# Similarity products of clustered attention: 32 instead of 128 columns of the centroids' tile

## The chip, the cores and the metric

One core of one Trainium2 chip. The metric is the device time in microseconds (us) of one execution; the median of three runs of the kernel before is 679.25 us (678.80 to 679.58).

## The reference

The model is clustered attention followed by two feed-forward blocks, all in float32. Batch 2, 8 heads, 768 tokens, head size 64, 16 centroids for each head.

```python
c_n = centroids / (norm(centroids) + 1e-06)
q_assign = argmax(einsum('bhsd,hcd->bhsc', q_n, c_n), axis=-1)
k_assign = argmax(einsum('bhsd,hcd->bhsc', k_n, c_n), axis=-1)
mask = q_assign[:, :, :, None] == k_assign[:, :, None, :]
scores = where(mask, scale * q @ k.T, -1e9)
attn = softmax(scores); attn_out = attn @ v
```

A token thus takes part only in the attention of its own cluster. The change touches only the products `q @ c_n` and `k @ c_n`, from which the largest of 16 similarities is picked. After the attention come a Fourier mixing over tokens and channels, a normalization, an MLP of width 2048, and a gated MLP of width 1024 with a convolution of three taps.

## The kernel before, in words

**Stages.** Attention fills the first 250 us or so of the span. The mixing of batch 0 and the first weights are woven into it; the MLPs follow, with the mixing of batch 1 beside them. The 16 head-batch pairs are taken two at a time: `m` (0 to 7) numbers the pairs, and one `raw` tile holds q and k of two heads, 64 partitions each.

**Order of the work.** The attention runs in an order written out by hand. A loop over steps `n` (L856) issues a score step for the maximum (`score_max`, L587 and L589: four matmuls of 384 columns), a second computation of the same scores for the exponential (`score_exp`, L624 and L626, four more), the product with V (`attn_v`, L664, 18 short matmuls), and whatever the dictionaries `pre`, `mid`, `late`, `aft`, `post` and `fill` list for that step. TensorE takes its matmuls in that order. Three PSUM slots (`slot`, L363) go round between score steps and everything else.

**The similarity products.** The tile `W` (L400) has 128 partitions, four pairs of heads and 128 columns. It is set to zero, and L424 and L425 copy the normalized centroids of one head into columns 0 to 15 (partitions 0 to 63) and those of the other head into columns 16 to 31 (partitions 64 to 127). Columns 32 to 127 stay zero. `prep_sims` (L442) makes twelve float32 matmuls for a pair: the stationary operand is a block of 128 tokens of q or k, the moving operand is `W[:, m % 4, :]`, and product `t` writes 128 columns of PSUM from column `32 * t`. The next product overwrites all but the first 32 of them, so that columns 0 to 383 end up with the similarities of the twelve blocks. `prep_equal` (L451) reads just those. In the trace a float32 matmul stands as two weight loads and two matmuls, 24 of each for one call.

**When.** Pairs 0 and 1 are done back to back before the loop (L836, L845). The transposes of the first head's mask follow (`first_mask`, L490, matmuls at L495), then the first score steps. `prep_sims` of pairs 2 to 7 is listed in `post` (L690), one call in every twelve steps. Its result goes through VectorE (L455, L457), GpSimd (L461) and VectorE again (L465, L471), back to TensorE to be turned (L483), and by DMA into the stacked operands of a later head. No DMA is issued by `prep_sims`.

**Other lines that the steps below touch.** `keep_warm` (L406) multiplies zeros and nothing reads its result: eight such matmuls of 512 columns stand ahead of the centroids' work (L410), two behind the transpose of the centroids (L422), and four at step -2 (L716). `scales` (L334) has the only other float32 matmuls with 32 moving columns or fewer; `first_max` (L612) turns the maxima of the first head.

Of the kernel before, what the change touches and what calls it, by code (L numbers as in the profile page):

```python
# [49 lines left out]
def tile_net(ctx, tc, qk, v, cen, w12, w34, conv, dft, odd, out):  # L50
    nc = tc.nc
    V, A, G, T = nc.vector, nc.scalar, nc.gpsimd, nc.tensor
# [302 lines left out]
    with ExitStack() as actx:  # L355
# [7 lines left out]
        def slot(name):  # L363
            turn[0] = (turn[0] + 1) % 3
            return ps.tile([128, 2, 512], F32, tag=f"s{turn[0]}", bufs=1, name=name)
# [34 lines left out]
        W = ep.tile([128, 4, 128], F32, name="W")  # L400
        V.memset(W, 0.0)
        t = slot("warm_up")
# [27 lines left out]
        for i in range(2):  # L430
            t = ap.tile([128, NT, 2, 130], F16, name=f"V16_{i}")
# [6 lines left out]
        def first_bank(name):  # L438

            return ps.tile([128, 512], F32, tag="av", bufs=2, name=name)  # L440

        def prep_sims(m):  # L442
            raw = raws[m]
            sm = sims[m] = first_bank("sim1") if m == 1 else slot(f"sim{m}")[:, 0]
            for t in range(12):
                T.matmul(sm[:, 32 * t:32 * t + 128], raw[:, t // 6, (t % 6) * 128:(t % 6) * 128 + 128],
                         W[:, m % 4, :], start=True, stop=True)
            if m != 1:
                prep_equal(m)

        def prep_equal(m):  # L451
            sm = sims[m]
            sv = sm[:, 0:384].rearrange("p (g h c) -> p h g c", g=12, h=2)
            mx = ep.tile([128, 2, 12], F32, tag="mx", bufs=1, name=f"mx{m}")
            V.tensor_reduce(mx, sv, AX.X, ALU.max)  # L455
            eq = eqs[m] = ep.tile([128, 24, C], F16, tag="eq", bufs=1, name=f"eq{m}")
            V.tensor_tensor(eq.rearrange("p (h g) c -> p h g c", h=2), sv,  # L457
                            mx.unsqueeze(3).to_broadcast([128, 2, 12, C]), ALU.is_equal)
# [227 lines left out]
        for m in range(1, NH // 2):  # L686
            k = 12 * m - 24
            if m > 1:
                at(pre, k, load_raw, m)
                at(post, k + 5, prep_sims, m)  # L690
                at(fill, k + 6, prep_first, m, V if m == 6 else G)
                at(fill, k + 7, prep_pick, m)
                at(fill if m == 7 else late, k + (7 if m == 7 else 8), prep_mark, m)
                at(fill, k + 8, prep_hi, m, (0,))
                at(fill, k + (9 if m < 7 else 8), prep_lo, m, 0, G if m < 7 else V)
                at(fill, k + (9 if m < 7 else 8), prep_hi, m, (1,))
                at(mid, k + 11, prep_turn, m)
                at(fill, k + (10 if m < 7 else 9), prep_lo, m, 1, G if m < 7 else V)
            turn_v = {1: 7, 6: 66, 7: 72}.get(m, k + 15)
            load, top, hi, lo = {1: (2, 5, 12, 13), 2: (8, 14, 17, 17), 6: (62, 64, 67, 71), 7: (68, 71, 74, 74)}.get(  # L700
                m, (k + 8, k + 13, k + 17, k + 17))
            at(fill, load, load_v, m)
            at(aft, top, v_max, m)
            at(mid, turn_v, v_turn, m)
            for i in range(4):
                if i:
                    at(aft, turn_v + (1 if 1 < m < 6 else i // 2), v_step, m, i)
                else:
                    at(late, turn_v, v_step, m, i)
            at(fill if m in (1, 6) else aft, hi, v_step, m, 4)  # L710
            at(pre if m == 6 else fill if m == 1 else aft, lo, v_step, m, 5)
# [122 lines left out]
        add_stack(G)  # L834
        first_stack()
        prep_sims(0)  # L836
        for h in range(2):
            parts[h] = stack_parts(h)
# [4 lines left out]
        prep_pick(0)  # L843
        prep_mark(0)
        prep_sims(1)  # L845
        A.copy(Ys[0][0:64, 0], f32(Gs[0][0:64, 0]))
        prep_hi(1)
# [231 lines left out]
    for g in range(B):  # L1079
        for f in range(16):  # L1080
# [7 lines left out]
            if g == 0 and f in (13, 14):  # L1088
                raw = cvs[0].tile([128, 2048], I32, tag="raw64", bufs=2, name=f"junk{f}")
# [102 lines left out]
```

## Time and profile before

| | us |
|---|---|
| Median of 3 runs (lowest, highest) | 679.25 (678.80, 679.58) |
| Profiled execution, device time | 679.98 |
| Span of that execution's profile | 678.2 |
| TensorE matmul (PE) busy | 662.7 (98%) |
| TensorE weight load (PEld) busy | 503.1 (74%) |
| VectorE (DVE) busy | 539.0 (79%) |
| ScalarE (ACT) busy | 417.5 (62%) |
| GpSimd (POOL) busy | 179.1 (26%) |

The device time is 1.78 us more than the span, the part ahead of the first and behind the last instruction. Matmuls are pipelined: the duration of one holds its way through the array as well as the time its columns take, so PE's busy share says little, and the distance between the starts of neighbours says more. PEclk is the granted clock, 1.00 for 2.4 GHz and 0.50 for 1.2 GHz. A bracket behind a row of the timeline gives the idle time of the engine just before it and what ended it.

### The profile page before, as it was taken

How to read it: one execution, taken by the hardware profiler on the slowest of the kernel's cores; microseconds unless marked ns; L12 is line 12 of the kernel's file. 1: busy time of each engine (PE TensorE's matmuls, PEld its weight loads, DVE VectorE, ACT ScalarE, POOL GpSimd, SP SyncE). 2: the span in 40 equal slices, each digit the busy share in tenths (PEclk: the TensorE clock that was granted, in tenths of full speed). 3: DMA queues.
4: the chain of work that ended last, by engine and by line, in shares of the span. 5: the costliest groups of instructions: out<-in, count | busy, mean ns of one | idle time of the engine just before them, and what ended most of it. 6: DMA issues, size and time to landing. Idle time of an engine off the chain costs nothing.

```text
span 678.2 us, 12781 instructions
## 1 busy us (share of the span) xinstructions
PE 662.7 (98%) x5114; PEld 503.1 (74%) x5114; DVE 539.0 (79%) x884; ACT 417.5 (62%) x671; POOL 179.1 (26%) x153
## 2 busy tenths in 40 slices
PE   8999999999999999999999999999999999999997
PEld 6798898988999888999999996555555555555553
DVE  6887889899889999998599848997626399867662
ACT  5577878888667885566246643776436276655442
POOL 8266757678648733000011000000000000000000
PEclk9999999999999999999999999999999999999999
DMA  7657797774643530334113330333000000002002
GB/s 203 166 137 191 187 226 196 199 181 90 170 112 90 140 125 1 126 124 143 45 63 125 125 125 1 124 125 127 1 0 1 1 0 1 1 2 93 1 1 93
DMA packets 21544, 65.42 MB, mean 96 GB/s; under 512 B 4439, under 2 KB 7307, under 8 KB 18669
## 3 DMA queue, kind: packets, MB, share of 16 engines
q1 hardware_dynamic: 20476, 60.86, 31.1%
q0 software_dynamic: 1008, 3.75, 2.0%
q8 instruction: 40, 0.66, 0.4%
q14 instruction: 20, 0.16, 0.1%
HBM read 40.84 MB, written 5.58 MB: 68 GB/s over the span
## 4 chain that ended last, share of the span: by engine, by line
PE 67%; DVE 21%; DMA 4%; ACT 3%; issue 3%; SPq 1%; POOL 1%; DVEq 0%; ACTq 0%
PE acc L87 7%; PE acc L86 7%; PE acc L85 7%; PE up L85 5%; PE up L86 5%; PE up L87 5%; PE av L664 4%; DVE m L592 3%; PE s L587 3%; PE t L624 3%; PE s L589 3%; PE t L626 3%; DVE p L652 3%; PE u L85 2%; PE u L87 2%
## 5 line engine op out<-in xcount | busy, mean ns | idle before, releaser
L652 POOL TENSOR_TENSOR p<-p,p 128x768 f16<-128x768 f32 x61 | 104.6, 1717 | 76.9 <-ACT p L644 35.0
L632 ACT ACTIVATE p<-t,cbias 128x768 f32<-128x768 f32 x93 | 83.6, 900 | 20.1 <-PE t L626 19.5
L592 DVE TENSOR_REDUCE m<-s 128x1 f32<-128x768 f32 x96 | 90.3, 945 | 7.0 <-PE s L589 4.6
L644 ACT CAST p<-p 128x768 f16<-128x768 f32 x90 | 74.7, 830 | 1.4
L664 PE MATMUL av<-V,p 128*128 128x65 f16 x1728 | 70.1, 194 | 1.0 <-POOL p L652 0.9
L664 PEld LDWEIGHTS <-p 128*128 128x128 f16 x1728 | 58.6, 98 | 16.2 <-issue 14.8
L587 PE MATMUL s<-X 128*128 128x384 f32 x192 | 56.1, 373 | 0.5 <-issue 0.4
L624 PE MATMUL t<-X 128*128 128x384 f32 x192 | 53.2, 358 | 0.9 <-DVE m L592 0.6
L589 PE MATMUL s<-Y 96*128 96x384 f32 x192 | 49.7, 340 | 2.1 <-DMA Y<-G 2.1
L626 PE MATMUL t<-Y 98*128 98x384 f32 x192 | 49.4, 338 | 0.0
L85 PE MATMUL u<-x,wb 128*128 128x384 f16 x128 | 41.7, 326 | 1.2 <-DVE h L955 0.8
L85 PE MATMUL up<-un,wa 128*128 128x384 f16 x128 | 41.8, 326 | 0.6 <-DVE x L1034 0.3
L86 PE MATMUL up<-un,wa 128*128 128x384 f16 x128 | 41.7, 326 | 0.0
L87 PE MATMUL u<-x,wb 128*128 128x384 f16 x128 | 41.7, 326 | 0.0
L86 PE MATMUL u<-x,wb 128*128 128x384 f16 x128 | 41.7, 326 | 0.0
L87 PE MATMUL up<-un,wa 128*128 128x384 f16 x128 | 41.6, 326 | 0.0
L652 DVE TENSOR_TENSOR p<-p,p 128x768 f16<-128x768 f32 x32 | 40.2, 1257 | 0.6 <-ACT p L644 0.5
L85 PE MATMUL up<-un,wha 128*128 128x384 f32 x112 | 38.0, 339 | 0.0
L86 PE MATMUL up<-un,wha 128*128 128x384 f32 x112 | 37.8, 338 | 0.0
L87 PE MATMUL up<-un,wla 128*128 128x384 f32 x112 | 37.6, 337 | 0.0
L589 PEld LDWEIGHTS s<-Y 96*128 96x128 f32 x192 | 34.8, 189 | 3.0 <-DMA Y<-G 1.6
L265 POOL TENSOR_TENSOR rs<-rs,half 128x1 f32<-128x1 f32 x12 | 10.5, 900 | 100.6 <-DVE rs L260 92.6
(388 smaller groups left out, 1710.7 us busy)
## 6 DMA issues: line engine op xcount, KB each, us to landing
rawa<-w SPq DMA_DIRECT2D x14, 1024.0 KB, 4.7
rawb<-w SPq DMA_DIRECT2D x8, 1024.0 KB
raw<-qk SPq DMA_DIRECT2D x7, 768.0 KB, 4.2
X<-G SPq DMA_DIRECT2D x13, 384.0 KB, 3.7
Y<-G SPq DMA_DIRECT2D x13, 384.0 KB, 6.8
vraw<-v SPq DMA_DIRECT2D x8, 384.0 KB, 4.9
out<-y SPq DMA_DIRECT2D x12, 256.0 KB, 2.0
X<-G SPq DMA_DIRECT2D x14, 192.0 KB, 4.2
```

The lines of the kernel that those rows point to most:

```text
L85: T.matmul(o, sH, mH, start=start, stop=False)
L86: T.matmul(o, sH, mL, start=False, stop=False)
L87: T.matmul(o, sL, mH, start=False, stop=stop)
L587: T.matmul(t[:, c, 0:384], X[:, 0, sl], X[:, 1, 384 * c:384 * c + 384], start=True, stop=False)
L589: T.matmul(t[:, c, 0:384], Y[0:96, 0, sl], Y[0:96, 1, 384 * c:384 * c + 384], start=False, stop=True)
L592: V.tensor_reduce(m6s[h][:, i:i + 1], t[:, :, 0:384], AX.XY, ALU.max, negate=True)
L624: T.matmul(t[:, c, 0:384], X[:, 1, sl], X[:, 0, 384 * c:384 * c + 384], start=True, stop=False)
L626: T.matmul(t[:, c, 0:384], Y[0:98, 1, sl], Y[0:98, 0, 384 * c:384 * c + 384], start=False, stop=True)
L632: A.activation(p, t[:, :, 0:384], AF.Exp, bias=cbias, scale=0.125)
L644: A.copy(p16[:, 0], p32s[n])
L652: eng.tensor_sub(p16[:, 1], p, p16[:, 0])
L664: T.matmul(o, p16[:, k, 128 * j:128 * j + 128], v16[:, i, h % 2, 65 * part:65 * part + 65], start=(i + j + k + part == 0), stop=(i == 5), ...
```

## The change

Each of the twelve products reads 32 columns of `W` instead of 128 and writes 32 columns of PSUM instead of 128. The stationary operand, the number of instructions, the tile `W`, its zeros, the PSUM tile and the order of the work stay as they are.

```diff
             for t in range(12):
-                T.matmul(sm[:, 32 * t:32 * t + 128], raw[:, t // 6, (t % 6) * 128:(t % 6) * 128 + 128],
-                         W[:, m % 4, :], start=True, stop=True)
+                T.matmul(sm[:, 32 * t:32 * t + 32], raw[:, t // 6, (t % 6) * 128:(t % 6) * 128 + 128],
+                         W[:, m % 4, 0:32], start=True, stop=True)
```

## Rows read from the trace of the kernel before

**Rows 1.** The page, part 2: granted clock in 40 slices of the span.
```profile
PEclk9999999999999999999999999999999999999999
```
**Rows 2.** The instructions of L446: duration ns min/median/max, first and last start.
```profile
L446 PEld LDWEIGHTS sim<-W,raw x168: 186/192/192, 6.2 to 188.5; 128*128 128x128 f32 x168
L446 PE MATMUL sim<-W,raw x168: 275/275/377, 6.2 to 188.6; 128*128 128x128 f32 x168
```
**Rows 3.** Chain of waits, 34.8 to 52 us: start, us, what.
```profile
35.43 2.76 PE sim L446 x24
38.19 0.35 PE s L587 x2
38.54 0.35 PE s L589 x2
...
39.58 0.57 PE av L664 x18
...
41.20 0.96 DVE m L592
```
**Rows 4.** Timeline around the batch at 35 us: start, us, instructions, idle before.
```profile
35.24 2.76 PEld L446 LDWEIGHTS sim<-W,raw 128*128 128x128 f32 x24
...
38.23 0.56 DVE L455 TENSOR_REDUCE mx<-sim 128x24 f32<-128x384 f32 x1 [2.25 <-PE sim L446]
```
**Rows 5.** Timeline around the matmuls of L334, float32 with 32 moving columns.
```profile
408.76 0.41 PEld L334 LDWEIGHTS sumsa<-sums,ones 128*128 128x128 f32 x2
408.99 0.30 PE L334 MATMUL sumsa<-sums,ones 128*128 128x32 f32 x2
409.10 0.19 PEld L85 LDWEIGHTS acc<-wha,hH 128*128 128x128 f32 x1
...
409.21 0.19 PEld L86 LDWEIGHTS acc<-wla,hH 128*128 128x128 f32 x1
```
**Rows 6.** The instructions of L334: duration ns min/median/max.
```profile
L334 PE MATMUL sumsa<-sums,ones x2: 191/232/274, 409.0 to 409.0; 128*128 128x32 f32 x2
```
**Rows 7.** Timeline of the first 22 us: the matmuls, and VectorE where it matters.
```profile
1.85 3.60 PE L408 MATMUL warm_up<-early 128*128 128x512 f16 x8 [1.85 <-DVE early L404]
...
6.17 2.94 PE L446 MATMUL sim<-W,raw 128*128 128x128 f32 x24
...
8.95 2.84 PE L446 MATMUL sim<-W,early 128*128 128x128 f32 x24
9.15 0.56 DVE L455 TENSOR_REDUCE mx<-sim 128x24 f32<-128x384 f32 x1 [1.34 <-PE sim L446]
...
12.01 1.51 PE L495 MATMUL fm<-ident,oh 128*16 128x128 f16 x24 [0.21 <-DVE oh L471]
...
15.03 5.27 DVE L592 TENSOR_REDUCE m<-s 128x1 f32<-128x768 f32 x6
...
20.37 0.58 PE L589 MATMUL s<-Y 96*128 96x384 f32 x2 [1.12 <-DMA Y<-G]
...
20.80 1.04 PE L408 MATMUL warm<-early 128*128 128x512 f16 x4
...
21.77 1.47 PE L612 MATMUL first_max<-ident,mh 128*2 128x128 f32 x12
```
**Rows 8.** The instructions of L408: duration ns min/median/max.
```profile
L408 PEld LDWEIGHTS <-early x14: 97/146/151, 1.8 to 21.2; 128*128 128x128 f16 x14
L408 PE MATMUL warm_up<-early x10: 380/634/634, 1.8 to 5.7; 128*128 128x512 f16 x10
L408 PE MATMUL warm<-early x4: 379/379/391, 20.8 to 21.5; 128*128 128x512 f16 x4
```
**Rows 9.** Busy time by stretch: length, then engines with counts, PEclk, DMA share, GB/s.
```profile
18.50:21.00 2.50, 1.38 (x7) 0.71 (x6) 2.14 (x6) 0.00 (x0) 0.00 (x0) 1.00 1.00 194
...
256.50:260.00 3.50, 2.58 (x49) 2.14 (x48) 3.50 (x8) 3.24 (x6) 2.00 (x2) 1.00 0.00 0
...
673.10:676.00 2.90, 0.00 (x0) 0.00 (x0) 1.14 (x2) 0.69 (x1) 0.00 (x0) 1.00 0.71 268
676.00:677.90 1.90, 0.00 (x0) 0.00 (x0) 0.00 (x0) 0.00 (x0) 0.00 (x0) 1.00 0.25 95
677.90:678.20 0.30, 0.00 (x0) 0.00 (x0) 0.00 (x0) 0.00 (x0) 0.00 (x0) 0.60 0.00 0
```

## Prediction

> **What bounds the kernel now.** I read the page first: TensorE is busy nearly all the time, and its granted clock stands at full in every one of 40 slices [rows 1]. Then the instructions of the changed line: 192 weight loads of 192 ns and as many matmuls of 275 ns, in eight batches of 24 [rows 2]; the 24 of pair 1, which read another tile, have the same durations. Then the chain of waits around one batch. It runs through TensorE without a gap: the batch (2.76 us), the score steps, the product with V; some us later VectorE takes over [rows 3]. So in the attention stage a microsecond given or taken on TensorE is mostly a microsecond of the kernel, and the edited line stands on the path six times. The other two batches lie at the start, from 6.2 us on [rows 2].
>
> **Part 1: shorter matmuls.** The edit cuts the moving columns to a quarter, but each matmul keeps its own load of 128 float32 columns. What sets the pace of a batch? The 24 loads take 2.76 us, the last one 0.19 of it, so they follow each other every (2.76 - 0.19) / 23 = 0.112 us [rows 4, 2]. The trace has one place with float32 loads of this size and 32 moving columns. There the two loads end at 409.17, so the second began at 408.98; the next loads begin at 409.10 and 409.21 [rows 5]. They are 0.12 and 0.11 us apart although a matmul with 32 columns stands between them. The matmul itself begins two or three hundredths after its neighbour, then takes 274 ns where the first takes 191 [rows 6]: it sits and waits for its weights. I conclude that the load holds the pace, before and after, and that the freed columns turn into time in which the array streams nothing.
>
> The gain of a batch is therefore 24 x (0.112 - 0.11), about 0.05 us. Its bounds: the hundredths of rows 5 leave 0.01 us a record either way, so 0.24 us gained or lost. Six batches on the path give -0.3 us (bounds -1.4 and +1.4). I take -0.3, by rows 5, the same form of instruction.
>
> The Trainium skill ("TensorE: Matmul & The Clock Gate", section "Back-to-back issue gap") has a formula by which the distance of isolated matmuls is columns / 2.4 plus 2.5 ns. By it, at two passes of 32 columns, a record would take 29 ns, and six batches would give 6 x 24 x (0.112 - 0.029) = -12 us; the section says too that in a stream of loads and matmuls both set the spacing, and rows 5 side with that.
>
> The last product is done 275 - 191 = 84 ns sooner [rows 2, 6], and VectorE waits for it: 1.34 us in the first batch, 2.25 us in the one at 35 us [rows 7, 4]. I cost this at nothing. At the start the first scores of the second head wait for a transfer until 20.37 [rows 7], and in the loop the next matmuls, not VectorE, follow on the chain [rows 3]. If that cover were gone it would be 0.08 us a batch. No wait, DMA or queue entry is added or moved.
>
> **Part 2: the granted clock.** 96 columns more make a matmul 84 ns longer [rows 2, 6], about two periods of 2.4 GHz a column. So 128 columns stream for some 107 of the 112 ns of a record: the array streams nearly all the time. Changed, it streams about 27 ns of every 110, a quarter. This lasts 2.7 us in a batch of the loop, and 5.35 us without a break at the start (two batches of 24 at 0.112).
>
> The trace shows both levels. The first eight matmuls of 512 columns take 634 ns each and come every (3.60 - 0.63) / 7 = 0.42 us, which is 512 columns at 1.2 GHz; the four at 20.80 take 379 ns and come every (1.04 - 0.38) / 3 = 0.22 us, at 2.4 GHz [rows 7, 8]. So the core started at the low level and left it after about 3.6 us of matmuls back to back. It fell again at the end: no matmul from 673.1 on, full clock until 677.9, 0.60 in the last 0.30 us [rows 9]. Between these lie stretches that held the full clock with TensorE partly idle: 1.38 us busy of 2.50 at 18.5 us, 2.58 of 3.50 at 256.5 us [rows 9]. Neither is as empty for as long as a changed batch, and the start, 5.35 us at a quarter, is longer than the silent 4.9 us after which the clock fell. No row shows a quarter, so whether the clock falls is the open question. I take it that it does, because the changed start lies nearer the row that fell than the rows that held.
>
> The Trainium skill (same page, "Part 1: The HAM clock gate") says that "the default state is throttled, and activity releases the throttle". That speaks against this change; rows 7 and 9 agree with it for full streaming and for silence, and no run here shows what lies between.
>
> What a fall costs at the start: the 24 transposes of the mask come every (1.51 - 0.22) / 23 = 0.056 us, 128 columns at 2.4 GHz; at the low level they take 24 x 0.053 = 1.3 us more [rows 7]. The row of six reductions behind them (15.03, 5.27 us) moves with them. But TensorE then stood 1.12 us waiting for a transfer that doesn't depend on the clock, and four matmuls of zeros stood ahead of L612 [rows 7]. So 0.3 us remain if these swallow most, 1.3 if they swallow nothing, and 2.6 if the second batch's loads slow as well, as the float16 loads did (146 against 97 ns [rows 8]: 24 x about 0.055 = 1.3 us). I take 0.8, between the first two, since the wait is in the row.
>
> What a fall costs in the loop: behind a batch come steps that stream nearly all the time [rows 3], so the clock should come back as it did at the start, after about 3.6 us, in which half the work is done: 1.8 us lost, or half of that where VectorE is the bound. I take 1.7 each, as the chain is TensorE's for six us behind the batch. How many of six? A batch is half as long as the stretch at the start and lies between dense steps, so none or all six are the ends; I take two, below the middle, since the stretches of rows 9 that held are of the same length.
>
> Sum: 0.8 + 2 x 1.7 - 0.3 = +3.9 us, against the profiled execution 679.98 + 3.9 = 683.9. That execution lies 0.73 above the median of the runs, so I put the median at 679.25 + 3.9 = 683.1.
>
> **Rivals.**
> *The clock holds* (not slower). A quarter of the columns may be enough to keep the full clock; TensorE goes on issuing as often as before. For it: the clock held at 18.5 and 256.5 us with TensorE idle for up to 1.1 us. Against: those stretches end sooner. It decides if no batch shows a clock under 1.00. Price: -0.3 us, so 678.9; its bounds are -1.4 and +1.4 us.
> *Only the start falls*. The batch is twice as long there, and batches of the loop have dense neighbours. Price: 0.8 - 0.3 = +0.5, so 679.8, with 0.3 to 2.6 for the start up to 681.6.
> *The pace follows the columns*. If the load is hidden after all, a record takes the 0.03 us between the two starts of L334's matmuls (0.30 - 0.27 us) [rows 5, 6], and six batches save 6 x 24 x 0.08 = 11.5 us: 667.7. Against it stands that the second of them waits 83 ns longer [rows 6].
> The edit certainly does what it says: the count of columns is in the instruction.
>
> **How the numbers follow.** A measurement of this kernel tells a difference of about 0.2%, 1.36 us, from none. Falls at the start and in the loop: 0.50, all of it slower by more. Only the start: 0.13, of which 0.10 within 0.2% and 0.03 slower. The clock holds: 0.32, of which 0.30 within and 0.02 faster. The pace follows the columns: 0.05, faster. So faster 0.07, same 0.40, slower 0.53. The likeliest case alone reaches from one fall in the loop (0.8 + 1.7 - 0.3 = +2.2: 681.4) to five (0.8 + 8.5 - 0.3 = +9.0: 688.2). The range takes in the rivals with a clock that holds: 678.7, a little under their 678.9, to 688.2. Outside lie the 0.05 of the fast rival, the outer part of the bounds, and six falls.
>
> **What would show it.** Right: the loads of L446 still about 0.11 us apart, its matmuls near 191 ns or longer where they wait; a granted clock under 1.00 in stretches after 6 us and just behind some of the batches at 35, 65, 94, 123, 152 and 186 us; matmuls of 384 columns there at twice their distance; each such stretch about 3.6 us. Wrong in part 1: loads much closer than 0.11 us, or a batch under 2.5 us. Wrong in part 2: a clock of 1.00 in all stretches, with a time within 1.4 us of before; or a clock that stays low for longer than 3.6 us, which would make it slower than I say.

## The result, and the profile after

The changed kernel takes 683.6 us (median of 20 runs, 679.06 to 688.4), the one before 679.05 (20 runs, 677.64 to 680.27): 1.0072 times as long, 95% interval 1.0054 to 1.0091, and the medians lie 4.55 us apart. (Here and below, a loss in us is the distance of two medians; the ratio and its interval are not the quotient of the medians, so the two can differ a little.) The prediction was 683.1, slower. The profiled execution of the changed kernel took 685.79 with a span of 684.0, 5.8 more than the span before.

The spread is part of the result: 9.3 us from the lowest to the highest run, where the kernel before has 2.6. The runs' mean granted clock goes from 0.997 in the fastest (679.06) to 0.985 in those of 685.79 and 687.22 us, and on the whole the longer runs are those with the lower mean clock; two don't fit, and come up under "What stays open".

The page's row of the granted clock in 40 slices, and the busy time of stretches (columns as in [rows 9]; the last three of a row are PEclk, DMA share and GB/s):

```profile
PEclk7999999999999999999999999999999999999999
```

```profile
6.00:8.64 2.64, 2.57 (x24) 2.60 (x24) 1.86 (x2) 2.64 (x4) 2.51 (x3) 1.00 0.29 119
8.64:18.88 10.24, 10.24 (x58) 9.96 (x58) 5.09 (x9) 4.97 (x7) 7.65 (x7) 0.50 0.95 222
70.08:73.49 3.41, 3.41 (x23) 3.11 (x23) 2.63 (x5) 1.82 (x3) 1.09 (x1) 0.50 0.97 205
100.80:104.20 3.40, 3.40 (x27) 3.09 (x27) 2.06 (x4) 2.89 (x4) 1.67 (x2) 0.50 1.01 209
```

The first slice is no longer full, against [rows 1]. The clock rose just ahead of the first batch, held through nearly all of it (to 8.64; its last load ends at 8.90), and then stood at 0.50, which is 1.2 GHz, for 10.24 us. It fell twice more, for 3.41 us each, right behind the batches at 67 and 97 us.

The instructions of L446, as in [rows 2]:

```profile
L446 PEld LDWEIGHTS sim<-W,raw x168: 186/192/295, 6.0 to 194.5; 128*128 128x128 f32 x168
L446 PE MATMUL sim<-W,raw x168: 268/276/403, 6.1 to 194.5; 128*128 128x32 f32 x168
L446 PEld LDWEIGHTS sim<-W,early x24: 333/333/333, 8.8 to 13.7; 128*128 128x128 f32 x24
```

The last of these rows in the kernel before:

```profile
L446 PEld LDWEIGHTS sim<-W,early x24: 192/192/192, 8.8 to 11.4; 128*128 128x128 f32 x24
```

A matmul of 32 columns still takes 276 ns where it used to take 275, since it waits for its weights as the one in [rows 6] does. The 24 loads of pair 1 take 333 ns each, where they took 192.

The timeline of the start, against [rows 7]:

```profile
6.04 2.86 PEld L446 LDWEIGHTS sim<-W,raw 128*128 128x128 f32 x24 [0.59 <-ACT W L425]
...
8.78 5.24 PEld L446 LDWEIGHTS sim<-W,early 128*128 128x128 f32 x24
...
14.09 2.73 PE L495 MATMUL fm<-ident,oh 128*16 128x128 f16 x24
...
16.75 1.01 PE L587 MATMUL s<-X 128*128 128x384 f32 x2
...
18.43 5.40 DVE L592 TENSOR_REDUCE m<-s 128x1 f32<-128x768 f32 x6 [0.63 <-PE s L589]
...
24.38 1.47 PE L612 MATMUL first_max<-ident,mh 128*2 128x128 f32 x12 [0.35 <-DVE mh L607]
```

The second batch's loads fill 5.24 us, where matmuls of the same batch took 2.84. They come every (5.24 - 0.33) / 23 = 0.213 us. So the mask's transposes begin at 14.09 instead of 12.01 and take 2.73 instead of 1.51 us, and the six reductions begin at 18.43 instead of 15.03, 3.4 us later. The slack behind them (the 1.12 us of waiting in [rows 7], which is gone) gives some of it back: L612 begins at 24.38 instead of 21.77. The start costs 2.6 us in this execution.

The timeline around a batch of the loop whose end meets a fall:

```profile
67.36 2.76 PEld L446 LDWEIGHTS sim<-W,raw 128*128 128x128 f32 x24
...
70.06 0.98 PE L587 MATMUL s<-X 128*128 128x384 f32 x2
...
71.47 0.84 PE L624 MATMUL t<-X 128*128 128x384 f32 x2
...
72.75 1.07 PE L664 MATMUL av<-V,p 128*128 128x65 f16 x18
...
73.66 0.60 PE L587 MATMUL s<-X 128*128 128x384 f32 x2
...
75.71 0.60 PE L587 MATMUL s<-X 128*128 128x384 f32 x2
```

The batch itself is 2.76 us of loads, to the hundredth as in [rows 4], and the next score step follows it 2.70 us behind its first load. In the kernel before, the same place reads:

```profile
65.35 2.76 PEld L446 LDWEIGHTS sim<-W,raw 128*128 128x128 f32 x24
...
68.06 0.60 PE L587 MATMUL s<-X 128*128 128x384 f32 x2
...
70.11 0.60 PE L587 MATMUL s<-X 128*128 128x384 f32 x2
```

There the score step follows 2.71 us behind the first load. So nothing is gained. From the score step at 70.06 to the next at 73.66 are 3.60 us; from there to the one at 75.71 it is 2.05, as between the two steps of the kernel before. This fall in the loop costs 1.55 us; the one at 100.80 us is spread over two steps, which take 5.65 us (100.18 to 105.83) where they took 4.14 in the kernel before (96.68 to 100.82): 1.5 us.

One wait more stands in this profile:

```profile
117.27 0.62 PE L626 MATMUL t<-Y 98*128 98x384 f32 x2 [1.39 <-DMA Y<-mr]
```

TensorE waits 1.39 us for the transfer that carries a head's maxima. The profile of the kernel before has no such wait. It isn't the clock's: the same wait stands in the profiles of two experiments below (3 and 6) whose clock was full in the loop. Whether the fewer columns bring it about is not shown: of the eleven profiles with fewer columns somewhere three have it and eight don't.

The sum for the profiled execution is 2.6 + 2 x 1.55 + 1.4 = 7.1 us, and 5.8 were measured. Half of the difference stands in one place, a wait of both kernels that is 0.6 us shorter after the change (the first row is before, the second after):

```profile
61.47 0.61 PE L589 MATMUL s<-Y 96*128 96x384 f32 x2 [0.94 <-DMA Y<-G]
63.46 0.62 PE L589 MATMUL s<-Y 96*128 96x384 f32 x2 [0.33 <-DMA Y<-G]
```

The rest is a few tenths in other places of the attention.

### The profile page after: what moved, and what is told of

The parts are those of the page before. It is cut to its first block, busy times and chain, and to the rows that moved or that the text cites. A ratio compares the mean times of both kernels' runs of the same rounds, so it can differ in the third digit from the quotient of the medians.

```text
span 684.0 us, 12781 instructions
## 1 busy us (share of the span) xinstructions
PE 669.1 (98%) x5114; PEld 510.6 (75%) x5114; DVE 539.8 (79%) x884; ACT 417.8 (61%) x671; POOL 178.8 (26%) x153
## 4 chain that ended last, share of the span: by engine, by line
PE 69%; DVE 22%; DMA 3%; ACT 3%; issue 2%; POOL 1%; SPq 0%; DVEq 0%; ACTq 0%
PE acc L85 7%; PE acc L87 7%; PE acc L86 7%; PE up L85 5%; PE up L86 5%; PE up L87 5%; PE av L664 4%; DVE m L592 4%; PE s L587 3%; PE sim L446 3%; PE s L589 3%; PE t L624 3%; PE t L626 3%; DVE p L652 3%; PE u L85 2%
## 5 line engine op out<-in xcount | busy, mean ns | idle before, releaser
L85 PE MATMUL u<-x,wb 128*128 128x384 f16 x128 | 41.7, 326 | 1.2 <-DVE h L955 0.9
L85 PE MATMUL up<-un,wa 128*128 128x384 f16 x128 | 41.8, 326 | 0.6 <-ACT wa L912 0.3
L85 PE MATMUL up<-un,wha 128*128 128x384 f32 x112 | 38.0, 339 | 0.0
L85 PE MATMUL acc<-wb,gH 128*128 128x512 f16 x96 | 36.4, 379 | 0.5 <-ACT gH L963 0.5
L626 PEld LDWEIGHTS t<-Y 98*128 98x128 f32 x192 | 35.5, 192 | 1.7 <-DMA Y<-mr 1.7
```

The source lines that it names most:

```text
L85: T.matmul(o, sH, mH, start=start, stop=False)
L626: T.matmul(t[:, c, 0:384], Y[0:98, 1, sl], Y[0:98, 0, 384 * c:384 * c + 384], start=False, stop=True)
```

## The experiments

**1. 128 columns at the start, 32 in the loop.**

```diff
-                T.matmul(sm[:, 32 * t:32 * t + 32], raw[:, t // 6, (t % 6) * 128:(t % 6) * 128 + 128],
-                         W[:, m % 4, 0:32], start=True, stop=True)
+                c = 128 if m < 2 else 32
+                T.matmul(sm[:, 32 * t:32 * t + c], raw[:, t // 6, (t % 6) * 128:(t % 6) * 128 + 128],
+                         W[:, m % 4, 0:c], start=True, stop=True)
```

> The batches of pairs 0 and 1 keep 128 columns, the six of the loop read 32. Theory (the granted clock): no stretch under 1.00 before 30 us; behind zero to three of the six batches of the loop a stretch of about 3.4 us at 0.50, each worth 0.9 to 1.8 us; median 680.0 to 682.5, and it differs from run to run by more than the kernel before does (2.6 us). Rival 1 (only the start costs): the same as before, 678.7 to 679.4. Rival 2 (each batch of 32 columns costs the same, whatever the clock): six eighths of 4.6 us, 682.4 to 682.6, with little spread.

Measured: 682.65 us (12 runs, 679.21 to 687.7) against 678.81, ratio 1.0052 (1.0034 to 1.0070), or 3.8 us. Busy time of the stretches at 0.50 in its profile:

```profile
37.86:41.27 3.41, 3.41 (x27) 3.11 (x26) 2.47 (x5) 1.13 (x2) 1.00 (x2) 0.50 1.00 206
68.58:71.99 3.41, 3.41 (x27) 3.10 (x26) 2.47 (x4) 2.19 (x3) 1.28 (x1) 0.50 1.03 196
99.30:102.70 3.40, 3.40 (x27) 3.09 (x26) 1.85 (x3) 3.12 (x4) 1.88 (x2) 0.50 1.01 207
```

Three of the six batches of the loop are followed by a fall, and the start by none. The time is a little over the 682.5 I gave as the upper end and lies at rival 2's value; but rival 2 wanted little spread, and this has 8.5 us. The batches still take 2.76 us of loads, and each of these stretches stands right behind one of them. Rival 1 is out. (A batch of 32 columns is called thin below, the matmuls of more columns around it dense.)

**2. 32 columns at the start, 128 in the loop.** The same edit with `32 if m < 2 else 128`.

> The batches of pairs 0 and 1 read 32 columns, the six of the loop keep 128. Theory: one stretch at 0.50 from about 8.6 us to 19 us in each run and none later; 2.0 to 2.8 us slower than before, so 681.1 to 681.9, with no more spread than before. Rival 1 (only the start costs): all of the loss of the changed kernel, 683.2 to 684. Rival 2: two eighths of 4.6 us, 680.2.

Measured: 680.68 us (10 runs, 678.75 to 682.61) against 678.81, ratio 1.0024 (1.0013 to 1.0034), or 1.9 us. Its profile is of a run of 679.37 us:

```profile
4.60:11.39 6.79, 6.56 (x53) 5.61 (x51) 5.09 (x9) 5.26 (x9) 6.50 (x15) 1.00 0.60 190
11.39:14.81 3.42, 3.23 (x27) 2.89 (x27) 1.83 (x3) 1.54 (x3) 3.31 (x4) 0.50 1.01 277
```

Here the clock held through both batches and fell only at 11.39 us, for 3.42 us, so the loads kept their pace and little was lost. This is a miss: 681.1 to 681.9 was expected, with the long stretch in each run and no more spread than before, and the runs spread over 3.9 us against 1.8. Their mean clock goes from 0.997 in the three fastest to 0.992 in the slowest: how long the clock is low, and with it the price, differs from run to run. Rival 2's 680.2 lies near; experiment 3 decides on it. Experiments 1 and 2 together make 5.7 us, where the changed kernel has 4.55 with an interval from 3.7 to 6.2: start and loop add up, within what can be told.

**3. 64 columns everywhere.** The same edit with `c = 64`.

> All eight batches read and write 64 columns. Theory: the loads still 0.112 us apart. If the array is full enough, the clock is 1.00 throughout and the time that of before, 678.7 to 679.4; if not, the same stretches at 0.50 as with 32 columns, fewer of them, and 680 to 683. Rival 2 (fewer columns cost by themselves, whatever the clock): two thirds of 4.6 us, 682.1, with a clock of 1.00.

Measured: 679.12 us (11 runs, 678.44 to 680.54), ratio 1.0003 (0.9994 to 1.0011). Its stretches, and a row of its waits in the loop (engine, what it waited for, us in total, times, longest):

```profile
7.05:35.00 27.95, 26.93 (x230) 23.67 (x229) 23.73 (x37) 17.74 (x25) 14.74 (x12) 1.00 0.66 167
35.00:200.00 165.00, 161.81 (x1879) 147.18 (x1879) 142.92 (x213) 127.47 (x175) 109.58 (x75) 1.00 0.68 172
```

```profile
PE t L627 <- DMA Y<-mr: 1.1, 1, 1.1
```

The clock is full throughout and the time is that of before. Half the columns cost nothing and bring nothing, so the loss isn't one of fewer columns as such, and rival 2, which wanted 682.1 with a full clock, is out. All eleven runs have a mean clock of 0.998 or more. The wait for the maxima (1.1 us) stands here too, with the clock at 1.00.

**4. 32 columns, and a filler behind each product.**

```diff
+                T.matmul(sm[:, 384:512], ident16, ident16, start=True, stop=True)
```

> All eight batches read 32 columns, and behind each of the twelve products stands one float16 product of 128 columns whose result is not read. Theory: the clock falls less often than with 32 columns alone or not at all; the fillers cost 0.03 to 0.06 us each, so 12 x 6 of them 2.2 to 4.3 us; together 681.2 to 683.4 if the clock holds. Rival 2: the fillers come on top of the changed kernel, 685.8 to 688.

Measured: 682.25 us (5 runs, 682.06 to 682.79), ratio 1.0048 (1.0036 to 1.0060), or 3.4 us. The clock was 1.00 in all stretches after its rise. Two rows of the timeline in a batch of the loop, the loads of two products that follow each other:

```profile
37.01 0.30 PEld L446 LDWEIGHTS sim<-W,raw 128*128 128x128 f32 x2
...
37.26 0.30 PEld L446 LDWEIGHTS sim<-W,raw 128*128 128x128 f32 x2
```

A product and its filler take 0.25 us, a product alone 2 x 0.112; the fillers of the loop cost 12 x 6 x 0.026 = 1.9 us. The profiled run, 2.8 us longer than the profiled run before, bears this out: the first matmul behind the last batch (L85) begins at 190.23 instead of 188.60, 1.6 us later. The other 1.1 us stand far from any filler: at L1031 (L1032 here), 484.48 instead of 481.73 us, all 2.8 are there. What brings them about is open. What matters for the theory is the clock, and with it the spread: 0.7 us in five runs, where the changed kernel has 9.3 in 20. With a filler behind each product the products of 32 columns lose nothing to the clock, and the kernel pays for the fillers instead. Rival 2, 685.8 to 688, is out.

**5 and 6. 32 columns in one batch of the start alone.** The same edit with `32 if m == 0 else 128` and `32 if m == 1 else 128`.

> Only the first batch (pair 0, behind the centroids' transpose) reads 32 columns; the thin stretch at the start lasts 2.7 us and dense products follow. Theory: the clock falls in fewer runs than in loop128, whose thin stretch is 5.35 us; median 678.8 to 680.0. Rival 3 (any batch of 32 columns at the start drops the clock, since the core has only just left the low level there): as loop128, 680.3 to 681.1.

> Only the second batch (pair 1) reads 32 columns; dense products stand ahead of it, the wait for the mask's transposes behind it. Theory: as with pair 0 alone or a little worse, since TensorE idles behind it; 678.8 to 680.3. Rival 3: 680.3 to 681.1.

Measured: 679.79 us for pair 0 (12 runs, ratio 1.0011, 1.0000 to 1.0022), four of them at 681.4 to 682.1 and the others under 680.3; 679.02 us for pair 1 (12 runs, ratio 0.9998, 0.9988 to 1.0008), two of them over 681. Rival 3's time, 680.3 to 681.1, was met by neither. Its mechanism isn't out: the profiled run of pair 1 has a fall, behind the thin batch and in the mask's transposes, and six of the twelve runs have a mean clock of 0.995 to 0.997.

```profile
12.26:15.67 3.41, 3.41 (x26) 3.20 (x24) 2.07 (x3) 1.98 (x3) 3.41 (x2) 0.50 1.03 269
```

```profile
21.79 1.47 PE L613 MATMUL first_max<-ident,mh 128*2 128x128 f32 x12 [0.35 <-DVE mh L608]
```

But this fall costs nothing: `first_max` begins at 21.79, where it began at 21.77 [rows 7]. One thin batch at the start can drop the clock; in this run no thin batch came into the low stretch, and the slack took the price. That run is still one of the long ones (681.76 us), by the wait for the maxima and not by its clock:

```profile
PE t L627 <- DMA Y<-mr: 1.5, 1, 1.5
```

**7. The loop's batches cut in two.** 128 columns at the start; in the loop six products of 32 columns ahead of the products with V, and six behind.

```diff
-                at(post, k + 5, prep_sims, m)
+                at(late, k + 5, prep_sims, m, range(6))
+                at(post, k + 5, prep_sims, m, range(6, 12))
```

> Start with 128 columns; in the loop each batch of 32 columns is cut in two halves of six products with the 18 products with V (0.57 us) between them. Theory: the thin stretch of 2.7 us becomes two of 1.35 us with dense work between, so the clock falls less often than in start128 (682.65); 679.0 to 681.5. Rival 4 (the number of thin products counts, wherever they stand): as start128, 682 to 683.3.

Measured: 679.6 us (11 runs, 677.68 to 682.01), ratio 1.0005 (0.9994 to 1.0016). The timeline of one batch:

```profile
34.01 1.42 PE L449 MATMUL sim<-W,raw 128*128 128x32 f32 x12
...
35.27 0.72 PE L667 MATMUL av<-V,p 128*128 128x65 f16 x18
...
35.82 1.50 PE L449 MATMUL sim<-W,raw 128*128 128x32 f32 x12
```

The same 72 products of 32 columns, 0.57 us of dense work between the halves, and the median is that of before, so rival 4 is out: not the number of thin products decides, but whether they stand in one stretch. The falls are rarer, not gone: the profiled run, the fastest of all, had a mean clock of 1.000, but four others have 0.995 or 0.996 and took 679.76 to 682.01 us.

**8. Four products of zeros between the two batches of the start.** The loop has 128 columns.

```diff
+            if m == 1:
+                for _ in range(4):
+                    T.matmul(sm, zero[:, 0:128], zero, start=True, stop=True)
```

> As loop128 (pairs 0 and 1 with 32 columns, the loop with 128), with four products of 512 columns of zeros (0.22 us each) between the two batches. Theory: the thin stretch of 5.35 us is broken in two of 2.7 us, and the clock falls in fewer runs; TensorE has 1 us of slack there, so 678.8 to 680.0. Rival 3: as loop128 plus up to 0.9 us, 680.7 to 681.6.

Measured: 682.65 us (12 runs), ratio 1.0034 (1.0013 to 1.0054). This is a miss: 678.8 to 680.0 was expected. The runs fall into two groups, five from 678.9 to 679.6 and seven from 682.6 to 685.2. The profile, of a run of 683.28, belongs to the second group. Two stretches, and the timeline of the zeros and of the second batch:

```profile
5.71:9.13 3.42, 3.42 (x28) 2.85 (x27) 2.13 (x3) 3.38 (x6) 3.29 (x3) 1.00 0.31 131
9.13:19.37 10.24, 10.24 (x56) 9.32 (x55) 4.59 (x8) 4.32 (x7) 6.33 (x7) 0.50 1.02 227
```

```profile
8.87 1.65 PE L447 MATMUL sim<-early 128*128 128x512 f16 x4
...
10.31 5.16 PE L450 MATMUL sim<-W,early 128*128 128x32 f32 x24
```

The clock fell at 9.13, at the end of the first batch; the zeros began at 8.87 and so ran at the low clock (1.65 us for four, 1.04 at full clock in [rows 7]), and the second batch took 5.16 us behind them. In this run they came too late for the fall and made its price higher. The other long runs are not all of this kind: five of the seven have a mean clock of 0.990 to 0.992, but the two longest, 685.06 and 685.21 us, have 1.000, and no profile shows what lengthened them. Experiment 5 doesn't help: of its four long runs two have a mean clock of 0.996 and 0.997 and two have 1.000, and its profile is of the shortest run, with a full clock.

**9. Fillers in the start alone.** 32 columns and the filler of experiment 4 for pairs 0 and 1, 128 columns in the loop.

> Loop with 128 columns; the two batches at the start read 32, with one float16 product of 128 columns, whose result is not read, behind each of the 24 products. Theory: the clock stays at 1.00 behind its rise in all or nearly all runs, so the loss of loop128 (1.9 us) and of gap4 (3.4 us) goes; the fillers (24 x about 0.047 us by the run with fillers everywhere) hide for the most part in TensorE's slack there: 678.8 to 680.3, and nothing over 681.5. Rival 5 (at the start 32 columns cost through the loads and the longer batches, not through the clock): gap4 or worse, 682 to 684.

Measured: 679.2 us (11 runs, 678.82 to 681.44), ratio 1.0002 (0.9993 to 1.0011).

```profile
6.10:14.00 7.90, 7.77 (x97) 7.45 (x96) 5.02 (x8) 6.22 (x10) 6.98 (x7) 1.00 0.66 184
14.00:670.00 656.00, 648.93 (x5022) 494.14 (x5023) 528.63 (x863) 407.70 (x657) 166.84 (x118) 1.00 0.33 93
```

The loss of experiments 2 and 8 is gone, with the same products of 32 columns, the same loads and longer batches. Rival 5 is out. All eleven runs have a mean clock of 0.998 or more. That the start's loss is the clock's is shown by this experiment together with the profiles of the changed kernel and of experiment 8, where the second batch takes about 5.2 us at the low level instead of 2.8.

**10. The changed kernel again**, nothing altered.

> The changed kernel once more, nothing altered, for a second profile. Theory: other places of the stretches at 0.50, each of 3.4 us or a multiple; 1.3 to 1.5 us lost in each of the loop, and a start between 0 and 3.5 us; median 682.7 to 684.5, lowest about that of before.

Measured: 684.43 us (9 runs, 680.56 to 691.35; 683.64 without the longest), ratio 1.0064 (1.0043 to 1.0086). Its profile:

```profile
7.06:10.47 3.41, 3.41 (x32) 3.41 (x32) 1.71 (x3) 3.06 (x5) 3.27 (x3) 1.00 0.32 72
10.47:17.30 6.83, 6.83 (x43) 6.55 (x43) 3.69 (x7) 3.23 (x5) 4.95 (x6) 0.50 1.02 246
126.53:129.94 3.41, 3.41 (x27) 3.10 (x26) 2.40 (x4) 2.29 (x4) 1.35 (x1) 0.50 0.99 203
157.25:160.66 3.41, 3.41 (x27) 3.10 (x26) 3.25 (x4) 0.85 (x1) 3.41 (x5) 0.50 0.93 203
```

Other places than in the first profile: the long stretch begins inside the second batch and lasts 6.83 us, and the falls of the loop stand behind the batches at 124 and 154 us. Again two of six. The price is smaller at the start: `first_max` begins at 23.46, 1.7 us later than before.

```profile
23.46 1.47 PE L612 MATMUL first_max<-ident,mh 128*2 128x128 f32 x12 [0.36 <-DVE mh L607]
```

The median is within what was expected; the lowest run is not, 2.1 us above the lowest of before (678.44).

**What stays open.** Two of the 20 runs of the changed kernel took 687.82 and 688.4 us with a mean clock of 0.993 and 0.995, and two of experiment 10 took 687.45 and 691.35 with 0.994 and 0.988. The lost clock that is recorded doesn't account for these, as little as for the two longest of experiment 8: a run with 0.995 elsewhere took 680.53, two with 0.988 took 684.6. The mean clock has a blind spot: it doesn't count the low level ahead of the first rise (the profile before has 1.000, and its first eight matmuls ran at 1.2 GHz). So a clock that rises late might lengthen a run without lowering its mean clock. Whether that happened is not shown, since none of these runs has a profile.

## Why the prediction was right

**The loads hold the pace: right.** Predicted was a gain of 0.05 us a batch; measured is 2.76 us of loads before and after, so 0.00, and the -0.3 of the sum was nothing. The rival in which the pace follows the columns is out. The formula that the Trainium skill gives for isolated matmuls ("TensorE: Matmul & The Clock Gate", section "Back-to-back issue gap") doesn't hold for this stream: an estimate by it is 29 ns a record, and the trace has 112.

**The clock falls: right**, at the start and behind two of the six batches in both profiles of the changed kernel, three in experiment 1. Two were taken; as the prediction says, that was a choice between none and six which no row fixed, so hitting it is in part luck. That the thin stretch is the reason is shown by experiments 4, 7 and 9, which leave products at 32 columns (all, those of the loop, those of the start) and break the thin stretch up, and by experiment 3, which keeps the stretch and gives it 64 columns.

**The price in the loop: right**, 1.55 us in the trace for 1.7, and 3.4 us of low clock for 3.6 in all falls of the loop.

**The price of the start: mis-sized.** I took 0.8 us, with 2.6 as the upper end "if the second batch's loads slow as well". They do: 0.213 us apart, where they should be 0.112. The step that failed is the one that took the loads as unharmed and gave the low clock 3.6 us where it lasted 10.24 in this profile; a clock that stays low for longer than 3.6 us was among the prediction's own signs of being wrong. Taking the wait for the transfer as cover was right: it gave back about 1 us. That the upper end of 2.6 is also what this profile shows is luck. It was 1.3 for the loads and 1.3 for the transposes, with nothing covered; measured are 5.24 - 2.76 = 2.5 us for the loads and 2.73 - 1.51 = 1.2 for the transposes, less the cover. The size for the loads came from float16 loads (146 against 97 ns), and float32 loads slow by more (333 against 192). Over many runs the start costs 1.9 (experiment 2), as in some the fall comes after the loads.

So the forecast of 3.9 us came near the 4.55 with one term too small by 1.1 to 1.8 and a gain of 0.3 that did not come. The sum with measured terms, 1.9 + 2 x 1.55 = 5.0, would have lain 0.45 too high, where the forecast was 0.65 too low. The 1.4 us of waiting for the maxima in the profiled execution belong to no term of the prediction.

**The rivals.** The clock held in one run of 20 at most, the one of 679.06 us: its mean clock of 0.997 is also that of experiment 2's profiled run, whose clock fell once for 3.4 us. That only the start falls is seen in neither profile of the changed kernel.

## What to carry to other kernels

Where weight loads hold the pace of a run of matmuls, columns taken out of the moving operand save no time; look at the distance of the loads before counting columns. Columns that seem wasted may keep the array busy, and a thin stretch of a few microseconds can cost twice: in the dense work behind it, and in its own loads. If a thin stretch can't be avoided, breaking it up with work that is needed anyway cost nothing that could be measured here (experiment 7). Fillers inside the stretch kept the clock (experiments 4 and 9); matmuls put behind its first half did not (experiment 8).

## What was not expected of the hardware

Float32 weight loads follow the granted clock: 128 columns every 0.112 us at 2.4 GHz and every 0.213 at 1.2. The Trainium skill (same page, section "LDWEIGHTS (loading the stationary operand)") gives columns / 1.2 ns, by which 128 columns are estimated at 107, and names no dependence on the clock; at full clock the trace agrees (112), at the low level it shows about twice as much (213).

The clock's stretches at 0.50 were 3.4, 6.8 or 10.2 us long in these profiles, and the same kernel had them in other places from run to run. So a kernel with a thin stretch shows it as spread between runs: 9.3 us here, against 2.6 before and 0.7 in the five runs with fillers everywhere. Not all of that spread is the clock's, as the runs under "What stays open" say.
